# Attention and two expert layers on one core: prologue and first sixteen steps written in another order

## The chip, the cores and the metric

The kernel runs on one core of a Trainium2 chip. The metric is the device time of that core in microseconds (us). Five engines have queues of their own: PE (matrix products), DVE (vector), ACT (activations), POOL, and SP, which here only issues DMAs.

## The reference

Attention over chunks of 32 queries feeds a gated layer and then a layer of eight experts. What the change touches is the attention and the first gated layer:

```python
scores = scale * np.matmul(q_c, k_full.transpose(0, 1, 3, 2))
scores = scores - np.max(scores, axis=-1, keepdims=True)
a = np.exp(scores)
a = a / (np.sum(a, axis=-1, keepdims=True) + 1e-09)
out[:, :, c_start:c_end] = np.matmul(a, v_full)
...
h = x @ w_in
relu6 = np.clip(h + 3.0, 0.0, 6.0)
g = h * relu6 / 6.0
return (g @ w_out).astype(np.float32)
...
for e in range(E):
    h = np.maximum(x @ w1[e], 0.0)
    ye = h @ w2[e]
    out += P[:, e:e + 1] * ye
```

Sizes: 4 batches, 8 heads, 768 positions, 64 per head; 3072 tokens of 512, a hidden layer of 2048 for the first gated layer, and eight experts with 1024 each.

## The kernel before

Attention is cut into 32 **units** u of 96 queries with all eight heads. A unit passes through: a_load and v_load (DMA), a_scores (PE, eight products into two PSUM tiles `sc` of four heads), a_max (DVE, the negated maximum `nm`), a_exp (ACT, eight exponentials, which also give the sums `sm`), a_norm (DVE, `sm`, `rc`, and a multiplication of all of `e`), a_transpose (PE into two PSUM tiles `pt`, ACT copies them to `et`), a_values (PE into `av`) and a_split (ACT `xh`, DVE `xl`: a high and a low part, since every large product is made in three passes). Four units are a block of 384 tokens.

The weights of the first layer arrive as raw 8-byte words and are converted on the core: single_act makes `rest` and `pw` on ACT, single makes `sa` or `sb` with four DVE instructions, single_hi makes the high part `wah`/`wbh` on ACT, and single_lo the low part `wal`/`wbl` on DVE. convert_act(n) holds the ACT half, convert(n) the DVE half (single_lo of what ACT has finished, then single of the next).

The gated layer runs in **steps** i. A step has first(i) (twelve products into `ph`, then `t` on ACT and again on DVE), first_parts(i) (`hh` on ACT, `hl` on DVE) and second(i - 2) (twelve products into four accumulators `pa`). The first 16 steps take two blocks with half the weights, then the same with the other half. Steps 0 to 3 carry a whole unit each; after that a unit is spread over three steps: **turn** marks the step with the transposes, **due** the next one with values, split, scores and maximum.

Everything stands under a manual schedule: each engine executes its instructions in the order in which the code is written. PSUM tiles `pt`, `av` and `sc` of the steps share two banks in turn (`ps_s`), so the second half of a unit's scores needs the bank that its predecessor's `av` held. After the attention, blocks are read back from DRAM by x_load and split by x_split, for the second pass over the layer (`pe` = 1), whose first step begins right after the last step of the first pass.

The prologue of before is:

```python
        for j in range(UPB + 2):
            a_scores(j, True)
            a_load(j + 2)
            if j >= 1:
                a_norm(j - 1)
            if j >= 2:
                a_split(j - 2)
            if j >= 1:
                convert_act(1)
            a_max(j)
            if 1 <= j <= UPB:
                a_transpose(j - 1)
                a_values(j - 1)
                v_load(j + 1)
            a_exp(j)
            convert(1)
```

Of the kernel before, what the change touches and what calls it, by code (L numbers as in the profile page):

```python
# [8 lines left out]
F32 = mybir.dt.float32  # L9
F32R = mybir.dt.float32r  # L10
U32 = mybir.dt.uint32
AF = mybir.ActivationFunctionType
# [5 lines left out]
NH = 8  # L18
# [20 lines left out]
def attn_moe_moe(ctx: ExitStack, tc: tile.TileContext, qk, vw, wi, wo, wa, wb, wg, out):  # L39
# [61 lines left out]
    def raw_load(n):  # L101
        pe, f, t = wide[n]
        raws[n] = at_p.tile([128, 2 * DM], U32, tag="raw", name="raw", bufs=RAW)
        nc.sync.dma_start(out=raws[n], in_=(wi if t == "a" else wo)[pe, f].bitcast(U32))
# [51 lines left out]
    def convert(n):  # L156

        for m in range(going[2], going[1]):
            single_lo(m)
        going[2] = going[1]  # L160
        for m in range(going[0], min(going[0] + n, len(wide))):
            single(m)
            if m + RAW < len(wide):
                raw_load(m + RAW)
            going[0] = m + 1

    def convert_act(n):

        for m in range(going[0], min(going[0] + n, len(wide))):
            single_act(m)  # L170
        for m in range(going[1], going[0]):
            single_hi(m)
        going[1] = going[0]
# [26 lines left out]
    def a_load(u):  # L200
        t = at_p.tile([D + 3, NH, UQ + UK], F32, tag="qk", name="qk", bufs=2)
        nc.sync.dma_start(out=t[:D], in_=qk[u, :D])
        nc.sync.dma_start(out=t[D:], in_=qk[u, D:])
        qk_t[u] = t

    def v_load(u):
        t = at_p.tile([UK, NH * D], F32, tag="vw", name="vw", bufs=2)
        nc.sync.dma_start(out=t, in_=vw[u])
        v_t[u] = t

    def a_scores(u, early=False):

        t = qk_t.pop(u)
        ps, tag = (ps_a, "a") if early else (ps_s, "s")
        sc_t[u] = sc = [ps.tile([UQ, 4, UK], F32, tag=tag, name="sc") for _ in range(2)]
        for h in range(NH):
            nc.tensor.matmul(sc[h // 4][:, h % 4, :], t[:, h, :UQ], t[:, h, UQ:], start=True, stop=True)

    def a_max(u):
        mx = sm_p.tile([UQ, NH], F32, tag="mx", name="mx")  # L220
        for j in range(2):
            nc.vector.tensor_reduce(out=mx[:, 4 * j:4 * j + 4], in_=sc_t[u][j], axis=AX.X, op=ALU.max)
        nm = sm_p.tile([UQ, NH], F32, tag="nm", name="nm")
        nc.vector.tensor_scalar_mul(nm, mx, -SCALE)
        e_t[u] = nm

    def a_exp(u):
        nm, sc = e_t[u], sc_t.pop(u)
        ef = at_p.tile([UQ, NH, UK], F32, tag="e", name="e", bufs=2)
        sm = sm_p.tile([UQ, NH], F32, tag="sm", name="sm")  # L230
        for h in range(NH):
            nc.scalar.activation(
                out=ef[:, h], in_=sc[h // 4][:, h % 4], func=AF.Exp, scale=SCALE, bias=nm[:, h:h + 1],
                accum_out=sm[:, h:h + 1])
        e_t[u] = ef, sm

# [27 lines left out]
    def a_split(u):  # L264
        ps = av_t.pop(u)
        b, i = divmod(u, UPB)
        if i == 0:
            xs[0, b] = x_tiles()
        s = slice(UQ * i, UQ * i + UQ)
        hi, lo = (t[:, :, s] for t in xs[0, b])  # L270
        split(hi, lo, ps)
        xf = at_p.tile([128, KT, UQ], F32, tag="xf", name="xf", bufs=3)
        nc.gpsimd.tensor_tensor(out=xf, in0=hi.bitcast(F32), in1=lo.bitcast(F32), op=ALU.add)
        spills.append((xd[b][:, i], xf))
# [3 lines left out]
    def spill():  # L278
        while spills:
            nc.sync.dma_start(out=spills[0][0], in_=spills.pop(0)[1])  # L280
# [442 lines left out]
    with tc.manual_schedule():  # L723
        at_ctx = pool("at", 2, side="right")
        at_p = at_ctx.__enter__()
        a_load(0)
        v_load(0)
        v_load(1)
        raw_load(0)
        a_load(1)  # L730
        for n in range(1, RAW):
            raw_load(n)
        make_identity(nc, ident)
        nc.gpsimd.memset(ones, 1.0)
# [2 lines left out]


        convert_act(1)
        for j in range(UPB + 2):  # L740
            a_scores(j, True)
            a_load(j + 2)
            if j >= 1:
                a_norm(j - 1)
            if j >= 2:
                a_split(j - 2)
            if j >= 1:
                convert_act(1)
            a_max(j)
            if 1 <= j <= UPB:  # L750
                a_transpose(j - 1)
                a_values(j - 1)
                v_load(j + 1)
            a_exp(j)
            convert(1)

        def rate(i):

            pe, b, f = steps[i]
            return 0 if pe or b == NB1 - 1 else int(i != 4 and i < 11) if i < 2 * NF else f % 2  # L760

        build = None
        jobs, begun = factory(), [0, 0, 0]
        xb_ctx = ctx.enter_context(ExitStack())
        for i, (pe, b, f) in enumerate(steps):


            if i < 4:
                u, turn, due = i + UPB, True, True
            elif i < 2 * NF:  # L770
                u, turn, due = (i - 4) // 3 + 2 * UPB, (i - 4) % 3 == 0, (i - 4) % 3 == 1
            else:
                u, turn, due = (i - 2 * NF) // 2 + 3 * UPB, i % 2 == 0, i % 2 == 1
            turn, due = (pe == 0 and w for w in (turn, due))
            if (pe, b, f) == (0, NB1 - 1, 0):
                at_ctx.__exit__(None, None, None)
                xo_p = ctx.enter_context(pool("xo", 1, side="right"))
            if (pe, b, f) == (1, 1, 0):
                three.close()
                xb_p = xb_ctx.enter_context(pool("xb", 1, side="right"))  # L780
            if (pe, b, f) == (1, NB1 - 1, 0):
                assert build is None and begun[2] == len(jobs)
                xb_ctx.close()
                two.close()
                w1s_p, w1r_p, w2s_p = (
                    ctx.enter_context(pool(n, 1, side="right")) for n in ("w1s", "w1r", "w2s"))
                w1_load(0)
                w2_load(0)
            if (pe, b) == (1, NB1 - 1):
                for do, j in {2: ((w1_hi, 0),), 3: ((w1_lo, 0), (w1_load, 1)), 6: ((w1_hi, 1),),  # L790
                              7: ((w1_lo, 1), (w1_load, 2))}.get(f, ()):
                    do(j)

            for stage_, late in ((2, 4.2), (0, 0), (1, 2)):
                while begun[stage_] < len(jobs) and FIRST_JOB + PERIOD * begun[stage_] + late <= i:
                    jobs[begun[stage_]][stage_]()
                    begun[stage_] += 1
            if pe == 0 and b == NB1 - 1:
                w_load(f)
                if f == 3:  # L800
                    x_load(0)
            if pe == 1 and f == 2:
                x2_load(b)
                if b + 1 < NB1:
                    x_load(b + 1)
            spill()
            first(i)
            if pe or due:
                first_parts(i)
            if turn and due:  # L810
                if i >= LAG:
                    second(i - LAG)
                stage(a_transpose, u)
            if due:
                stage(a_values, u)
                stage(a_split, u)
                convert_act(rate(i))
                stage(v_load, u + 2)
            if i >= LAG and not (turn and due):
                second(i - LAG)  # L820
            if due:
                stage(a_scores, u + 2)
                stage(a_max, u + 2)
                stage(a_exp, u + 2)
                stage(a_load, u + 4)
                stage(a_norm, u + 1)
            if pe == 0 and not due:
                if turn:
                    stage(a_transpose, u)
                first_parts(i)  # L830
                convert_act(rate(i))
            if pe == 0:
                convert(rate(i))
            if later and f in (3, 5, 7):
                gate(*later.pop(0))
            if pe == 0 and b == NB1 - 1 and f >= LAG:
                w_split(f - LAG)
            elif pe == 1 and b == 0 and f < LAG:
                w_split(NF - LAG + f)

            n = b + 1 if pe else 0
            if f >= 4 and n < NB1 and (pe or b == NB1 - 1):
                x_split(n, f - 4)
            if (pe, b, f) == (1, 4, 0):
                build = x_ops(0, xb_p, "xb")
            if build:
                build = build if next(build, 0) is None else None
# [159 lines left out]
```

## Time and profile before

| what | us |
|---|---|
| median of 3 runs | 2633.09 (2632.29 to 2634.93) |
| span of the profiled execution | 2632.3 |
| first product of step 0, step 1, step 4, step 17 (from the span's start) | 42.4, 54.4, 87.2, 167.5 |
| PE busy over the span | 2565.9 |

The span runs from the first instruction to the last. The fastest run took 2632.29 us, so the profiled execution's own time is taken as its span, with nothing worth counting around it. Idle time matters where PE is idle, since PE is busy for 97% of the span; idle time of the others matters only where PE waits for it.

### The profile page before, as it was taken

What the parts mean: (1) busy time and instruction counts of PE and PEld (TensorE: products, weight loads), DVE (VectorE), ACT (ScalarE), POOL (GpSimd) and SP (SyncE); (2) the same over time, 40 slices, a digit from 0 to 9 for tenths busy, and PEclk for the clock granted to TensorE, in tenths of its full rate; (3) what the DMA queues carried; (4) which work ended last, traced back from release to release, by engine and by line L of the source; (5) the groups of instructions that cost most, each with busy time, mean ns of one, the idle gap of its engine ahead of it and who ended that gap; (6) DMA issues with size and microseconds to landing.
All of it is one profiled execution on the core that took longest, in us unless ns stands there. A gap on an engine that the chain in (4) does not pass through costs nothing.

```text
span 2632.3 us, 34096 instructions
## 1 busy us (share of the span) xinstructions
PE 2565.9 (97%) x12725; PEld 2217.9 (84%) x12725; DVE 2140.0 (81%) x2283; ACT 1385.9 (53%) x2323; POOL 1086.1 (41%) x692
## 2 busy tenths in 40 slices
PE   8999999999999999999989999999989999999997
PEld 7899999999977888888868888888868888888886
DVE  6768766556478999998987999998887888898887
ACT  6656654122245555555556555555555655555553
POOL 1034455443005645444433545453433344444442
PEclk9899999999999999999999999999999999999999
DMA  7468868675222443433333334333243333232322
GB/s 201 124 211 266 284 214 278 221 244 192 87 94 92 136 130 112 129 105 107 123 122 119 127 122 136 122 117 106 97 150 110 114 112 98 91 112 98 112 82 75
DMA packets 159702, 366.89 MB, mean 139 GB/s; under 512 B 14352, under 2 KB 75984, under 8 KB 159536
## 3 DMA queue, kind: packets, MB, share of 16 engines
q1 hardware_dynamic: 159536, 364.72, 43.1%
q8 instruction: 100, 1.64, 0.3%
q14 instruction: 66, 0.54, 0.1%
HBM read 297.45 MB, written 67.21 MB: 139 GB/s over the span
## 4 chain that ended last, share of the span: by engine, by line
PE 88%; DVE 6%; DMA 2%; ACT 2%; issue 1%; POOL 1%; SPq 0%; ACTq 0%; DVEq 0%
PE ga L193 6%; PE ga L192 6%; PE ga L194 6%; PE oa L193 6%; PE oa L194 6%; PE oa L192 6%; PE pa L192 3%; PE ph L192 3%; PE oc L193 3%; PE oc L194 3%; PE oc L192 3%; PE ph L193 3%; PE ph L194 3%; PE gc L193 3%; PE gc L192 3%; PE gc L194 3%
## 5 line engine op out<-in xcount | busy, mean ns | idle before, releaser
L637 POOL TENSOR_TENSOR g<-g,pb 128x512 f32<-128x512 f32 x368 | 768.6, 2106 | 1117.4 <-ACT g L630 971.3
L665 ACT ACTIVATE oh<-g 128x1024 fp32r<-128x1024 f32 x336 | 355.3, 1058 | 530.0 <-PE oa L194 178.5
L670 DVE TENSOR_TENSOR ol<-g,oh 128x1024 fp32r<-128x1024 f32 x336 | 493.8, 1481 | 71.4 <-ACT oh L665 71.2
L658 DVE TENSOR_TENSOR g<-g 128x1024 f32<-128x1024 f32 x188 | 323.2, 1752 | 17.9 <-POOL g L637 17.9
L192 PE MATMUL ga<-xo,w1h 128*128 128x512 f32 x768 | 302.3, 394 | 10.3 <-DVE g L624 5.4
L193 PE MATMUL ga<-xo,w1h 128*128 128x512 f32 x768 | 301.0, 392 | 7.2 <-DVE xo L181 7.2
L193 PE MATMUL oa<-ol,w2h 128*128 128x512 f32 x768 | 300.6, 391 | 4.8 <-DVE ol L670 4.8
L192 PE MATMUL oa<-oh,w2h 128*128 128x512 f32 x768 | 300.2, 391 | 0.6 <-ACT oh L665 0.6
L194 PE MATMUL ga<-xo,w1l 128*128 128x512 f32 x768 | 300.1, 391 | 0.0
L194 PE MATMUL oa<-oh,w2l 128*128 128x512 f32 x768 | 300.0, 391 | 0.0
L592 DVE TENSOR_TENSOR w2l<-w2s,w2h 128x1024 fp32r<-128x1024 f32 x168 | 264.6, 1575 | 27.9 <-ACT w2h L586 26.7
L586 ACT ACTIVATE w2h<-w2s 128x1024 fp32r<-128x1024 f32 x168 | 177.6, 1057 | 141.8 <-DMA w2s<-in_wb_dram 76.3
L568 DVE TENSOR_TENSOR w1l<-w1s,w1h 128x1792 fp32r<-128x1792 f32 x96 | 219.0, 2281 | 0.3
L630 ACT ACTIVATE g<-g 128x512 f32<-128x512 f32 x288 | 175.7, 621 | 74.2 <-DVE g L624 73.8
L455 POOL TENSOR_TENSOR fs<-fr 128x256 f32<-128x256 f32 x128 | 110.7, 865 | 212.8 <-DMA ws<-fs 210.0
L306 ACT ACTIVATE t<-ph,half 128x384 f32<-128x384 f32 x128 | 74.5, 582 | 235.2 <-PE ph L194 231.5
L307 DVE SCALAR_TENSOR_TENSOR t<-t,ph 128x384 f32<-128x384 f32 x128 | 70.6, 552 | 139.4 <-ACT t L306 139.3
L192 PE MATMUL ph<-xh,wah 128*128 128x384 f32 x512 | 182.1, 356 | 0.8 <-ACT xh L176 0.8
L192 PEld LDWEIGHTS ga<-xo,w1h 128*128 128x128 f32 x768 | 144.9, 189 | 42.3 <-ACT cp L615 6.2
L193 PE MATMUL ph<-xl,wah 128*128 128x384 f32 x512 | 176.0, 344 | 2.5 <-DVE xl L181 2.4
L193 PEld LDWEIGHTS ga<-xo,w1h 128*128 128x128 f32 x768 | 144.9, 189 | 38.7 <-DVE xo L181 9.5
L193 PEld LDWEIGHTS oa<-ol,w2h 128*128 128x128 f32 x768 | 144.8, 189 | 36.9 <-DVE ol L670 6.8
(140 smaller groups left out, 5904.0 us busy)
## 6 DMA issues: line engine op xcount, KB each, us to landing
w1s<-ws SPq DMA_DIRECT2D x96, 512.0 KB, 4.2
w2s<-ws SPq DMA_DIRECT2D x96, 512.0 KB, 3.9
w1s<-in_wa_dram SPq DMA_DIRECT2D x96, 384.0 KB, 3.1
w2s<-in_wb_dram SPq DMA_DIRECT2D x144, 256.0 KB, 3.3
ws<-fs SPq DMA_DIRECT2D x64, 512.0 KB, 5.8
fr<-in_wa_dram SPq DMA_DIRECT2D x32, 512.0 KB, 5.5
fr<-in_wb_dram SPq DMA_DIRECT2D x32, 512.0 KB, 4.8
qk<-in_qk_dram SPq DMA_DIRECT2D x32, 448.0 KB, 7.9
```

Source lines behind the costliest of these rows:

```text
L192: nc.tensor.matmul(ps, wh, xh, start=start, stop=False, skip_group_check=more)
L193: nc.tensor.matmul(ps, wh, xl, start=False, stop=False, skip_group_check=more)
L194: nc.tensor.matmul(ps, wl, xh, start=False, stop=stop, skip_group_check=more)
L455: nc.gpsimd.tensor_tensor(out=s[o], in0=a, in1=b, op=f)
L568: nc.vector.tensor_tensor(out=lo, in0=w1s.pop(j), in1=w1[j].bitcast(F32), op=ALU.subtract)
L586: nc.scalar.activation(out=hi, in_=w2s[m], func=AF.Copy)
L592: nc.vector.tensor_tensor(out=lo, in0=w2s.pop(m), in1=w2[m].bitcast(F32), op=ALU.subtract)
L630: nc.scalar.activation(out=g, in_=g, func=AF.Relu)
L637: nc.gpsimd.tensor_tensor(out=g, in0=g, in1=p, op=ALU.mult)
L658: eng.tensor_tensor(out=o, in0=gq[n, x, i], in1=gq[n, y, i], op=ALU.subtract)
L665: nc.scalar.activation(out=hi, in_=gq[n, b, i], func=AF.Copy)
L670: nc.vector.tensor_tensor(out=lo, in0=gq[n, b, i], in1=op[m, i].bitcast(F32), op=ALU.subtract)
```

## The change

In the prologue the scores of unit j + 1 are issued before the work on unit j - 1; the maximum of unit j and its exponentials stand ahead of the normalisation of unit j - 1; convert_act now comes behind the exponentials and the transposes, and a_split comes at the end, for unit j - 1 rather than j - 2. The maximum and its scaling are made for each half of the heads apart. Steps 0 to 15 get a function of their own, early. In the last block of the first pass, x_load(0) stands two steps earlier and each x_split one step earlier. The first DMAs have another order.

```diff
     def a_max(u):
-        mx = sm_p.tile([UQ, NH], F32, tag="mx", name="mx")
+        e_t[u] = []
         for j in range(2):
-            nc.vector.tensor_reduce(out=mx[:, 4 * j:4 * j + 4], in_=sc_t[u][j], axis=AX.X, op=ALU.max)
-        nm = sm_p.tile([UQ, NH], F32, tag="nm", name="nm")
-        nc.vector.tensor_scalar_mul(nm, mx, -SCALE)
-        e_t[u] = nm
+            mx = sm_p.tile([UQ, 4], F32, tag="mx", name="mx", bufs=4)
+            nc.vector.tensor_reduce(out=mx, in_=sc_t[u][j], axis=AX.X, op=ALU.max)
+            nm = sm_p.tile([UQ, 4], F32, tag="nm", name="nm", bufs=4)
+            nc.vector.tensor_scalar_mul(nm, mx, -SCALE)
+            e_t[u].append(nm)
...
+        a_scores(0, True)
+        a_load(2)
         for j in range(UPB + 2):
-            a_scores(j, True)
-            a_load(j + 2)
+            a_max(j)
+            a_exp(j)
+            if j < UPB + 1:
+                a_scores(j + 1, True)
+                a_load(j + 3)
             if j >= 1:
                 a_norm(j - 1)
-            if j >= 2:
-                a_split(j - 2)
-            if j >= 1:
-                convert_act(1)
-            a_max(j)
             if 1 <= j <= UPB:
                 a_transpose(j - 1)
                 a_values(j - 1)
                 v_load(j + 1)
-            a_exp(j)
+            if j >= 1:
+                convert_act(1)
             convert(1)
+            if 1 <= j <= UPB:
+                a_split(j - 1)
...
+        def early(i, u, turn, due):
+
+
+            if i < UPB:
+                if i:
+                    a_exp(u + 1)
+                convert(rate(i))
+                first(i)
+                a_transpose(u)
+                a_norm(u + 1)
+                if i >= LAG:
+                    second(i - LAG)
+                a_values(u)
+                a_split(u)
+                first_parts(i)
+                convert_act(rate(i + 1))
+                v_load(u + 2)
+                a_scores(u + 2)
+                a_load(u + 4)
+                a_max(u + 2)
+                return
+            if i == UPB:
+                a_exp(u + 1)
+            if due:
+                a_values(u)
+                a_split(u)
+                v_load(u + 2)
+                a_norm(u + 1)
+            convert(rate(i))
+            first(i)
+            first_parts(i)
+            convert_act(rate(i + 1))
+            second(i - LAG)
+            if due:
+                a_scores(u + 2)
+                a_max(u + 2)
+                a_exp(u + 2)
+                a_load(u + 4)
+            if turn:
+                a_transpose(u)
...
+        convert_act(rate(0))
...
-                if f == 3:
+                if f == 1:
                     x_load(0)
...
             spill()
+            if i < 2 * NF:
+                early(i, u, turn, due)
+                continue
             first(i)
...
-            if f >= 4 and n < NB1 and (pe or b == NB1 - 1):
-                x_split(n, f - 4)
+            r = f - (4 if pe else 3)
+            if 0 <= r < KT and n < NB1 and (pe or b == NB1 - 1):
+                x_split(n, r)
```

The queue of ACT in the prologue, unit j = 2, before: `rest`, `pw` and `wah` are the conversions, `et` the copies of the transposes, `e` the exponentials.

```order
L176 ACTIVATE xh_317<-av_270 128x4x96
L114 ACTIVATE rest_323<-raw_179 128x512
L116 ACTIVATE pw_325<-raw_179 128x512
L139 ACTIVATE wah_327<-sa_293 128x512
L252 ACTIVATE et_334<-pt_335 128x384
L252 ACTIVATE et_334<-pt_341 128x384
L232 ACTIVATE e_358,sm_359<-sc_300,nm_332 96x128 x4
L232 ACTIVATE e_358,sm_359<-sc_301,nm_332 96x128 x4
```

The same queue at the end of unit j = 2 and the beginning of j = 3 in the changed kernel:

```order
L253 ACTIVATE et_360<-pt_367 128x384
L114 ACTIVATE rest_384<-raw_179 128x512
L116 ACTIVATE pw_386<-raw_179 128x512
L139 ACTIVATE wah_388<-sa_312 128x512
L176 ACTIVATE xh_319<-av_373 128x4x96
L233 ACTIVATE e_411,sm_412<-sc_343,nm_405 96x128 x4
L233 ACTIVATE e_411,sm_412<-sc_344,nm_409 96x128 x4
```

The conversions moved from ahead of their unit's exponentials to behind them, with the split's `xh` behind them in turn.

The queue of DVE for j = 2 in the changed kernel: `mx` and `nm` are the maximum, `sm`, `rc` and `e` the normalisation of unit 1, `wal` to `sb` the conversion, `xl` the split of unit 1.

```order
L223 TENSOR_REDUCE mx_325<-sc_263 96x4
L225 TENSOR_SCALAR nm_327<-mx_325 96x4
L223 TENSOR_REDUCE mx_329<-sc_264 96x4
L225 TENSOR_SCALAR nm_331<-mx_329 96x4
L240 TENSOR_SCALAR sm_254<-sm_254 96x8
L242 RECIPROCAL rc_357<-sm_254 96x8
L243 TENSOR_TENSOR e_253<-e_253,rc_357 96x1024
L149 TENSOR_TENSOR wal_390<-sa_312,wah_388 128x512
L125 TENSOR_SCALAR pw_386<-pw_386 128x512
L126 TENSOR_SCALAR sb_392<-pw_386 128x512
L128 SCALAR_TENSOR_TENSOR sb_392<-raw_179,sb_392 128x512
L130 TENSOR_TENSOR sb_392<-sb_392,rest_384 128x512
```

`wal` reads the `wah` that ACT now makes behind the exponentials of j = 2, and the next maximum stands behind the conversion and `xl`; before, the normalisation and `xl` led and the maximum stood directly ahead of the conversion.

The queue of ACT in step 7 (a turn step), before:

```order
L306 ACTIVATE t_1207<-ph_1194,half_95 128x384
L252 ACTIVATE et_1222<-pt_1223 128x384
L252 ACTIVATE et_1222<-pt_1229 128x384
L315 ACTIVATE hh_1235<-t_1207 128x384
L114 ACTIVATE rest_1239<-raw_885 128x512
L116 ACTIVATE pw_1241<-raw_885 128x512
L139 ACTIVATE wah_1243<-sa_1187 128x512
```

And step 7 in the changed kernel:

```order
L307 ACTIVATE t_1255<-ph_1242,half_95 128x384
L316 ACTIVATE hh_1258<-t_1255 128x384
L114 ACTIVATE rest_1262<-raw_928 128x512
L116 ACTIVATE pw_1264<-raw_928 128x512
L139 ACTIVATE wbh_1266<-sb_1235 128x512
L253 ACTIVATE et_1280<-pt_1281 128x384
L253 ACTIVATE et_1280<-pt_1287 128x384
L176 ACTIVATE xh_1088<-av_1293 128x4x96
```

The copies `et` moved from ahead of `hh` and the conversions to behind them. On PE the products first(8) stood between the transposes and the values before; now the values come directly behind the transposes.

## Rows read from the trace of the kernel before

**Rows 1.** The page: span, and the busy time of the engines.

```profile
span 2632.3 us, 34096 instructions
...
PE 2565.9 (97%) x12725; PEld 2217.9 (84%) x12725; DVE 2140.0 (81%) x2283; ACT 1385.9 (53%) x2323; POOL 1086.1 (41%) x692
```

**Rows 2.** Windows: stretch, length, busy PE, PEld, DVE, ACT, POOL, clock, DMA.

```profile
6.00:43.00 37.00, 33.93 (x193) 30.53 (x193) 29.89 (x58) 28.78 (x109) 2.98 (x3) 1.00 0.86 233
...
88.00:168.00 80.00, 74.54 (x482) 72.42 (x481) 52.41 (x98) 46.30 (x146) 13.18 (x16) 0.92 0.49 151
...
430.00:450.00 20.00, 16.75 (x81) 16.18 (x80) 14.50 (x19) 7.82 (x15) 10.72 (x13) 0.83 0.85 298
```

**Rows 3.** Timeline of PE, prologue and steps: start, duration, instruction, idle before.

```profile
32.41 3.73 PE L217 MATMUL sc<-qk 67*96 67x128 f32 x16
36.12 1.51 PE L251 MATMUL pt<-ident,e 96*128 96x96 f32 x8
...
39.05 3.73 PE L217 MATMUL sc<-qk 67*96 67x128 f32 x16
...
43.14 0.69 PE L193 MATMUL ph<-xl,wah 128*128 128x384 f32 x1
...
54.38 0.67 PE L192 MATMUL ph<-xh,wah 128*128 128x384 f32 x1
...
87.16 0.67 PE L192 MATMUL ph<-xh,wah 128*128 128x384 f32 x1
...
167.52 0.42 PE L192 MATMUL ph<-xh,wah 128*128 128x384 f32 x1
```

**Rows 4.** Timeline at the end of the first pass: PE and DVE.

```profile
436.32 0.69 PE L193 MATMUL ph<-xl,wah 128*128 128x384 f32 x1 [2.42 <-DVE xl L181]
...
441.93 0.34 PE L192 MATMUL ph<-xh,wah 128*128 128x384 f32 x1
...
435.20 1.07 DVE L181 TENSOR_TENSOR xl<-xl,xh 128x384 fp32r<-128x384 f32 x1
```

**Rows 5.** Timeline of DVE: a maximum in the prologue, then a whole step.

```profile
10.59 0.17 DVE L224 TENSOR_SCALAR nm<-mx 96x8 f32<-96x8 f32 x1
...
42.54 0.55 DVE L181 TENSOR_TENSOR xl<-av,xh 128x384 fp32r<-128x384 f32 x1
...
54.77 0.69 DVE L222 TENSOR_REDUCE mx<-sc 96x4 f32<-96x512 f32 x1 [1.02 <-PE sc L217]
55.49 0.17 DVE L224 TENSOR_SCALAR nm<-mx 96x8 f32<-96x8 f32 x1
...
57.14 0.68 DVE L149 TENSOR_TENSOR wal<-sa,wah 128x512 fp32r<-128x512 f32 x1
...
60.00 0.55 DVE L307 SCALAR_TENSOR_TENSOR t<-t,ph 128x384 f32<-128x384 f32 x1
61.13 0.56 DVE L318 TENSOR_TENSOR hl<-t,hh 128x384 fp32r<-128x384 f32 x1 [0.59 <-ACT hh L315]
```

**Rows 6.** Timeline of ACT in the prologue: exponentials, conversions, copies of transposes.

```profile
10.86 0.36 ACT L232 ACTIVATE e<-sc,nm 96x128 f32<-96x128 f32 x1 [0.56 <-DVE nm L224]
...
13.62 0.68 ACT L114 ACTIVATE rest<-raw 128x512 uint32<-128x512 uint32 x1
...
34.53 0.69 ACT L114 ACTIVATE rest<-raw 128x512 uint32<-128x512 uint32 x1
...
35.65 0.64 ACT L139 ACTIVATE wah<-sa 128x512 fp32r<-128x512 f32 x1
...
37.03 1.13 ACT L252 ACTIVATE et<-pt 128x384 f32<-128x384 f32 x2 [0.73 <-PE pt L251]
38.06 0.35 ACT L232 ACTIVATE e<-sc,nm 96x128 f32<-96x128 f32 x1
```

**Rows 7.** Timeline of PE in step 6 at full clock: twelve products.

```profile
102.63 0.33 PE L192 MATMUL pa<-hh,wbh 128*128 128x384 f32 x1
...
104.71 0.33 PE L192 MATMUL ph<-xh,wah 128*128 128x384 f32 x1
```

More of the change, by code (lines that the diff above doesn't have):

```diff
@@ L232, in a_exp @@
             nc.scalar.activation(
-                out=ef[:, h], in_=sc[h // 4][:, h % 4], func=AF.Exp, scale=SCALE, bias=nm[:, h:h + 1],
+                out=ef[:, h], in_=sc[h // 4][:, h % 4], func=AF.Exp, scale=SCALE, bias=nm[h // 4][:, h % 4:h % 4 + 1],
                 accum_out=sm[:, h:h + 1])
@@ L726, in attn_moe_moe @@
         a_load(0)
+        a_load(1)
+        raw_load(0)
         v_load(0)
+        raw_load(1)
         v_load(1)
-        raw_load(0)
-        a_load(1)
-        for n in range(1, RAW):
+        for n in range(2, RAW):
             raw_load(n)
```

## Prediction

> **What bounds the kernel now.** The page comes first: PE is busy for 97% of the span [rows 1], so time is won or lost only where PE idles or runs at its lower clock. The windows by stage say where that is: 3.1 us of idle PE in the prologue's 37, 5.5 between 88 and 168, and 3.3 between 430 and 450, where the granted clock is 0.83 [rows 2]; elsewhere PE is full. The timeline of PE gives the pace: in the prologue one unit follows the other by 6.64 us (scores at 32.41 and 39.05), step 0's second product starts at 43.14, step 1 at 54.38, step 4 at 87.16, step 17 at 167.52 [rows 3]. The change acts on nothing behind that but the end of the first pass [rows 4]. So I work out when the changed kernel reaches these marks.
>
> **The prologue.** The rows of order show a loop through two queues that was not there. ACT makes a unit's weight parts (`rest`, `pw`, `wah`) behind its exponentials; DVE's conversion waits for them; the next maximum stands behind the conversion; and the next exponentials wait for that maximum. One turn of the loop, from maximum to maximum:
> half a maximum to `nm` 0.72, `nm` to the first exponential 0.27 [rows 5, 6], eight exponentials 2.76 [rows 6]: 3.75. Meanwhile DVE has done both halves (0.80 each with the small scaling) and the normalisation (1.57, from 55.49 to 57.14 less 0.08 for the scaling [rows 5]), at 3.17; the transposes start some 0.23 later (an estimate: the end of the multiplication and one semaphore), and `et` 0.91 after them (36.12 to 37.03 [rows 3, 6]), at 4.31, so ACT waits 0.56. Then `et` 1.03, `rest` and `pw` 1.12, `wah` 0.65 [rows 6], `wal` and the conversion 2.86 (57.14 to 60.00), `xl` 0.5 [rows 5]. Sum: 10.47 us a unit instead of 6.64. Halving the maximum saves 0.8 of this loop and costs one scaling (0.08 taken; nothing to 0.17, its row's length [rows 5]).
>
> The first maximum of unit 1 comes earlier than now, when DVE has converted the first weight: 10.59 + 0.08 + 2.26 = 12.9 (2.86 less 0.60 for `wal`). The loads are in another order, but the first weight still has about a megabyte of others ahead of it, by the tiles' sizes (two loads of `qk` in place of one and two of `vw`), so I count nothing for that, and 1 us either way for the range. Four turns later, at 12.9 + 41.9 = 54.8, the split of unit 3 is done, and step 0 can start in earnest: 43.14 becomes 54.9, **+11.7**.
>
> **Step 0.** It begins with what the prologue left behind, one after the other: maximum and exponentials of unit 5 (3.75, to 58.6), `rest`, `pw` and a high part (1.77, to 60.3), `wal` and conversion on DVE (2.86, to 63.2), the high part of that (0.65, to 63.8), again 2.86 (to 66.7), `t` 0.55, the normalisation 1.57 and `xl` 0.55 (to 69.4). `xl` frees the bank which the second half of unit 6's scores needs; half of 3.73 [rows 3] later, at 71.2, step 1 starts: 54.38 becomes 71.2, **+16.8** in all.
>
> **Steps 1 to 3.** Here the change helps: the exponentials no longer wait behind this step's scores. Step 1 I take with PE at the lower clock, 1.2 GHz, since it idles before the values of step 0: twelve products at 0.33 (17 from 436.32 to 441.93 [rows 4]) 4.0, transposes 1.5 and scores 3.7 [rows 3], values as the transposes 1.5: 10.7, less a little overlap 10.6. At 2.4 GHz it would be 7.4. Steps 2 and 3 at 2.4 GHz: the exponentials end 3.1 after the scores and free the bank of the second transposes (0.3), second 2.1 (twelve products from 102.63 to 104.71 [rows 7]), values 0.9 (as the transposes of 1.5, at twice the clock), `xh` and `xl` 1.1, half the scores 0.9, semaphores 0.2: 8.6. Sum 27.8 instead of 32.8, **-5.0**; step 4 starts at 99.0.
>
> **Steps 4 to 16.** What stalls now is scores that wait for the bank of `av`, because `xl` stands late on DVE; that goes, with the 5.5 us of idle PE [rows 2]. In its place `et` is late: in a turn step ACT now copies the transposes behind `hh` and the conversions, and PE has nothing between transposes and values. The longest case, from first(5) to first(8): `xh`, `xl` and normalisation 2.7; conversion on DVE 2.3; `t` to `hh` 0.6 (half of the 1.13 from `t` to `hl` [rows 5]); `hh` and the conversions of ACT 2.1; copying four accumulators 1.6 (0.4 each, an estimate by the two copies of `et`); exponentials 2.76; `t` on both engines, to `hh` 1.2; `hh` to the end of the high part 2.2; `wal` and conversion 2.86; `t` to `hh` 0.6; `hh` and conversions 2.1; the first `et` 0.5; values 0.9: 22.4. By the same walk first(4) to first(5) is 7.2, first(8) to first(11) 20.5, where the first product of a new accumulator also waits for the copy, and first(11) to first(17), where no weights are converted, 31.2. Sum 81.3 against 80.4 now [rows 3], **+0.9**. The floor is PE's own work: 13 steps of 24 products at 0.173 are 54.1, and four units' transposes, values and scores at 3.1 are 12.5: 66.6. Work of DVE in the 13 steps is less than that (46), so it sets no bound.
>
> **The end of the first pass.** Now the last `xl` ends at 436.27 and PE has waited for it [rows 4]; 3.25 us of the window are idle [rows 2], and 17 products run at 0.33 instead of 0.173, 2.7 more. With the load two steps and each split one step (over 4 us) earlier, the last `xl` is done near 431, ahead of the eleventh product of that step, which wants it. On SP the load passes two steps' weight loads; its tile is free and its source was written long before, so they are not held up. **-5.9**, at worst 0.
>
> **Sum.** 16.8 - 5.0 + 0.9 - 5.9 = +6.8: 2632.3 + 6.8 = 2639.1 for a profiled execution. The fastest run before equals the span; the median is 0.8 above it, so the median of the changed kernel is forecast at **2639.9**, 0.26% slower.
>
> One rule is weighed here. On ACT a conversion starts at 13.62, right when the eighth exponential is through [rows 6]; I read both queues as strictly in order. The Trainium skill says the same (TensorE: Matmul & The Clock Gate, "Engine queue depths" in Part 1): of the engines only PE reorders, and then only weight loads; ACT and DVE are strict FIFO. Were it otherwise, a conversion could pass the waiting exponentials, the unit would stay at 6.64, and the sum would be 15 us lower, near 2624. The rule speaks against this order of the code.
>
> **The rivals.**
> (a) The values do not wait in steps 4 to 16, because ACT is through with `hh` and conversions when the transposes end. Then PE sets the pace: 66.6 instead of 81.3, and 2639.9 - 14.7 = 2625, faster. The idle DVE in the present steps speaks for it, the chain of waits above against it. It decides the sign where these 13 steps fall below 69; between 69 and 79.9 they leave the whole within 0.2% (5.3 us), which is about what a measurement of this kernel can tell from no change.
> (b) PE stays at 1.2 GHz beyond step 1, or falls back to it after the wait of step 8. A step 2 at that clock is 14.1 instead of 8.6 (4.0 + 1.5 + 4.0 + 1.5 + 3.7, less 0.6 of overlaps): 2645, and up to 2648 with some of step 8. The clock after the wait of only 2.42 us in rows 4 speaks for it. The Trainium skill (same page, "HAM oscillation") has waits that recur and put the array back to the lower clock each time; the trace agrees with 0.33 a product there.
> (c) The earlier split does not help, because DVE is behind in that stretch anyway: 2639.9 + 5.9 = 2646. Its `xl` takes 1.07 there against 0.55 in the prologue [rows 4, 5]; against it, the whole row of splits moves by a step.
>
> **Chances.** The walk as forecast 50% (0.36 slower by over 0.2%, 0.14 within); its 13 steps partly relieved 23% (within); (a) in full 8% (faster); (b) 13% and (c) 6% (slower). Faster 0.08, same 0.37, slower 0.55. The range must reach into the relieved case (3 to 10 us less) and into (b): 2631 to 2648; it leaves out (a) and the far end of (b). The likeliest case alone is 2636 to 2643: step 1 at 2.4 GHz takes 3.2 off, and small errors of the walk are of like size.
>
> **What would show it.** In the profile after: DVE idle by some 3.9 us in each prologue unit before `wal`, with ACT as releaser, and ACT idle as long before the exponentials; units 10.5 apart; step 0's second product near 55, step 1 near 71, step 4 near 99, step 17 near 180; PE waiting 4 to 6 us for `et` before the values of unit 9; no wait for `xl` at the start of the second pass. The prediction is wrong if the prologue's pace stays below 8 (then all falls by 10 or more), or if the 13 steps take 70 or less.

## The result and the profile after

The changed kernel takes **2659.19 us** (median of 4 runs, 2656.40 to 2662.07), the kernel before, on the same chip, 2632.69: the ratio of the runs is **1.0107** (95%: 1.0094 to 1.0120). The forecast was 2639.9 with a range up to 2648: the direction is right, the size is 19 us off. The profiled execution is the longest of the four runs (2662.07).

The page of the changed kernel, span and busy time of the engines; PE is busy 7 us longer than in [rows 1]:

```profile
span 2660.3 us, 34174 instructions
...
PE 2572.8 (97%) x12725; PEld 2215.6 (83%) x12725; DVE 2138.8 (80%) x2315; ACT 1388.6 (52%) x2323; POOL 1083.5 (41%) x692
```

Timeline of PE in the changed kernel: first units, step 0's second product, the first products of steps 1, 2 and 4, the values of unit 9 with two products behind them, and step 17:

```profile
18.73 3.70 PE L217 MATMUL sc<-qk 67*96 67x128 f32 x16 [5.58 <-DMA qk<-in_qk_dram]
22.22 1.49 PE L252 MATMUL pt<-ident,e 96*128 96x96 f32 x8
...
32.91 1.51 PE L252 MATMUL pt<-ident,e 96*128 96x96 f32 x8 [4.05 <-DVE e L243]
...
43.62 1.51 PE L252 MATMUL pt<-ident,e 96*128 96x96 f32 x8 [3.99 <-DVE e L243]
...
54.33 1.51 PE L252 MATMUL pt<-ident,e 96*128 96x96 f32 x8 [3.99 <-DVE e L243]
...
61.50 0.69 PE L193 MATMUL ph<-xl,wah 128*128 128x384 f32 x1 [2.38 <-DVE xl L181]
...
78.34 0.67 PE L192 MATMUL ph<-xh,wah 128*128 128x384 f32 x1
...
85.87 0.42 PE L192 MATMUL ph<-xh,wah 128*128 128x384 f32 x1
...
103.89 0.42 PE L192 MATMUL ph<-xh,wah 128*128 128x384 f32 x1
...
133.26 1.55 PE L261 MATMUL av<-et,vw 128*64 128x96 f32 x16 [5.97 <-ACT et L253]
...
135.22 0.52 PE L193 MATMUL ph<-xl,wah 128*128 128x384 f32 x1
135.54 0.52 PE L194 MATMUL ph<-xh,wal 128*128 128x384 f32 x1
...
186.77 0.42 PE L192 MATMUL ph<-xh,wah 128*128 128x384 f32 x1
```

Read against [rows 3], unit follows unit by 10.71 us in place of 6.64, with PE waiting 4 us for the normalised exponentials each time, and the first unit's transposes (22.22) stand on PE behind scores that waited 5.58 us for a load. The values of unit 9 wait 6 us for `et`.

Timeline of DVE and of ACT in the changed kernel, one wait of each in the prologue: DVE's conversion waits for ACT's `wah`, and ACT's exponentials wait for DVE's `nm`.

```profile
36.62 0.69 DVE L149 TENSOR_TENSOR wal<-sa,wah 128x512 fp32r<-128x512 f32 x1 [3.85 <-ACT wah L139]
...
41.16 0.36 ACT L233 ACTIVATE e<-sc,nm 96x128 f32<-96x128 f32 x1 [4.20 <-DVE nm L225]
```

What PE waited for in the first 700 us of the changed kernel (total, times, longest):

```profile
PE av L261 <- ACT et L253: 14.2, 6, 6.0
PE pt L252 <- DVE e L243: 12.0, 3, 4.1
PE sc L217 <- DMA qk<-in_qk_dram: 11.6, 2, 6.0
PE sc L217 <- DVE xl L181: 3.3, 5, 1.8
```

Windows of the changed kernel, columns as in [rows 2]: the change from the first pass to the second (the product that starts at 436.32 in [rows 4] starts here at 452.14), the way from the second pass to the expert layers, and a stretch of the expert layers.

```profile
450.00:480.00 30.00, 30.00 (x175) 30.00 (x174) 20.53 (x33) 11.19 (x22) 17.68 (x20) 1.00 0.77 267
...
700.00:790.00 90.00, 88.89 (x458) 79.42 (x458) 52.71 (x116) 30.08 (x46) 0.00 (x0) 0.96 0.22 74
...
1000.00:1200.00 200.00, 200.00 (x878) 165.03 (x877) 180.58 (x156) 111.70 (x138) 94.66 (x46) 1.00 0.34 113
```

And the same stretch of the expert layers in the kernel before:

```profile
1000.00:1200.00 200.00, 200.00 (x884) 165.62 (x883) 182.80 (x156) 111.74 (x138) 92.94 (x45) 1.00 0.35 112
```

In both PE is busy all the time at full clock, and yet 878 products are made in place of 884. The groups by line, in that stretch of the changed kernel (busy, mean ns of one); before, each of these means is 389. These are the lengths of the records, which overlap: 200 us for 884 products is one every 226 ns.

```profile
L194 PE MATMUL oa<-oh,w2l 128*128 128x512 f32 x86 | 33.8, 392 | 0.0
L192 PE MATMUL oa<-oh,w2h 128*128 128x512 f32 x86 | 33.6, 391 | 0.0
L193 PE MATMUL oa<-ol,w2h 128*128 128x512 f32 x86 | 33.5, 389 | 0.0
```

The lag of the changed kernel behind the one before is found by pairing equal instructions of both traces, the n-th with the n-th. It is 19.25 us at step 17 (186.77 less 167.52), 13.8 after the end of the first pass, 17.1 where ACT makes the first `w2h` of the expert layers, and 28.6 near the end. Two fifths of the loss (11.5 of 28.0) thus arise where the diff changes no instruction.

### The profile page after: what moved, and what is told of

The parts are those of the page before. It is cut to its first block, busy times and chain, and to the rows that moved or that the text cites. A ratio compares the mean times of both kernels' runs of the same rounds, so it can differ in the third digit from the quotient of the medians.

```text
span 2660.3 us, 34174 instructions
## 1 busy us (share of the span) xinstructions
PE 2572.8 (97%) x12725; PEld 2215.6 (83%) x12725; DVE 2138.8 (80%) x2315; ACT 1388.6 (52%) x2323; POOL 1083.5 (41%) x692
## 4 chain that ended last, share of the span: by engine, by line
PE 88%; DVE 6%; ACT 3%; DMA 2%; issue 1%; POOL 0%; SPq 0%; ACTq 0%; DVEq 0%
PE ga L194 6%; PE ga L192 6%; PE ga L193 6%; PE oa L194 6%; PE oa L193 6%; PE oa L192 6%; PE gc L194 3%; PE gc L192 3%; PE oc L194 3%; PE gc L193 3%; PE oc L192 3%; PE oc L193 3%; PE pa L192 3%; PE ph L192 3%; PE pa L194 3%; PE pa L193 3%
## 5 line engine op out<-in xcount | busy, mean ns | idle before, releaser
L671 DVE TENSOR_TENSOR ol<-g,oh 128x1024 fp32r<-128x1024 f32 x336 | 487.2, 1462 | 76.7 <-ACT oh L666 76.6
```

What stands on the lines that cost most here:

```text
L671: nc.vector.tensor_tensor(out=lo, in0=gq[n, b, i], in1=op[m, i].bitcast(F32), op=ALU.subtract)
```

## The experiments

Theory A said: the halves of `mx` and of `nm`, four buffers of 16 bytes for each that take 32 bytes a buffer, put all tiles behind them at the left end of SBUF 128 bytes further (`w2h` from 3808 to 3936), and that makes products slower. Rivals: the expert layers go slower because they start later, or because of the order of instructions. Theory B: the rest is the prologue's loop and the first unit.

**Addresses alone.** pad_only is the kernel before with the shift and nothing else; after_old_addr is the changed kernel without the shift.

```diff
+    sm_p.tile([UQ, 16], F32, tag="pad", name="pad")      # pad_only
     ident = const.tile([128, 128], F32, name="ident")
```
```diff
-            mx = sm_p.tile([UQ, 4], F32, tag="mx", name="mx", bufs=4)
+            mx = sm_p.tile([UQ, 4], F32, tag="mx", name="mx")      # after_old_addr; nm too
```

> The kernel before, with 128 more bytes per partition reserved in the pool of small tiles, so that the tiles behind it stand where the changed kernel has them; no instruction moves. In the expert layers the changed kernel loses about 11.5 us in 1800 although PE waits no longer there: each third product takes a few ns more. Theory A (the shift of the tiles by 128 bytes does it): about 11 to 12 us slower than before, mean product of the expert layers 391 ns. Theory B (the order or number of PE's instructions does it): no change, 389 ns. Theory C (it is the run or the chip, not the kernel): 389 ns and no change here, and the changed kernel at its old addresses may show either.

> The changed kernel with two buffers in place of four for the halved maximum and its scaling, so that all other tiles stand at the addresses of before. Theory A (addresses): the expert layers run as before (389 ns a product), and the time is some 11 us below the changed kernel's: near 2647. Theory B (instructions): near 2659 and 391 ns. The first 190 us should be those of the changed kernel in either case (step 17 near 187).

pad_only: 2642.62 us, ratio 1.0041 (1.0028 to 1.0054); its lag is -0.2 at the start of the expert layers and grows evenly to 11.7. after_old_addr: 2646.38, ratio 1.0054 (1.0041 to 1.0068), and 884 products in the window again; its lag is 14.3 from the end of the first pass to the start of the expert layers and 13.6 at their end. So the shift costs 11.0 us by pad_only (2642.62 less the 2631.63 of the kernel before, measured beside it) and 12.8 by after_old_addr (2659.19 less 2646.38). The order of the code costs 14.8 (2646.38 less 2631.63) or the 13.7 that are left of 26.5. Theory A holds.

**What about the address.** Three other shifts of the kernel before, by the same line with other sizes; then 32 bytes that move only tiles of the expert layers (all those at the left end, or those behind the second weights); and 32 bytes at the left with 224 at the right.

```diff
-        w2r_p, g_p, op_p, y_p, pb_p, tmp_p, out_p = (
+        w2r_p, pad_p, g_p, op_p, y_p, pb_p, tmp_p, out_p = (      # pad_32_behind
...
+        pad_p.tile([128, 8], F32, tag="pad", name="pad")
```
```diff
+    sm_p.tile([UQ, 8], F32, tag="pad", name="pad", bufs=1)      # pad_both
+    ctx.enter_context(pool("padr", 1, side="right")).tile([128, 56], F32, tag="padr", name="padr")
```

> The kernel before with one unused tile of 32 bytes ahead of all others, so that the tiles behind it stand 32 bytes further (with 128 bytes the span was 10.5 us longer, products 391/389/392 ns instead of 389). Theory of alignment: the pace of products hangs on where a tile begins within some block of bytes; 32 bytes bring the weights from 3808 to 3840, a multiple of 256, so that the pace is another than at 128, as before or faster: 2625 to 2633. Rival, the distance: what counts is that the tiles stand nearer to or further from those at the right end, which don't move; then any shift is slower, 32 bytes by a part of it or by the whole: 2634 to 2643.

> The same with 256 bytes. If the place of a tile within 256 bytes (or a divisor of it above 128) decides: products at 389, the time that of before, 2630 to 2633. If the place within 512 bytes decides, or the distance to the tiles at the right end: products at 391 or another pace, 2638 to 2650.

> The same with 512 bytes. If the place of a tile within 512 bytes or within a divisor of it decides: products at 389, 2630 to 2633. If the distance to the tiles at the right end decides: slower than with 128 bytes or the same, 2640 or more.

> The kernel before with the unused 32 bytes only in the expert layers, ahead of all their tiles at the left end. If the slower products come from tiles of the expert layers: slower by 20 us, 2648 to 2655, as with 32 bytes ahead of everything. If from the small tiles ahead of them (the identity, the half, the routing's rows): 2630 to 2633.

> The same, with the 32 bytes behind the second weights (w2h, w2l), so that these stay at 3808 and g, oh, ol, y and what follows move. If the second weights against the tiles at the right end decide: as before, 2630 to 2633. If the moved operands oh and ol, or what DVE, ACT and POOL write, decide: slower, 2640 to 2655. If only the difference between tiles that are used together counts, oh against w2h now differ as well, and it may be slower than with 32 bytes ahead of all.

> The kernel before with 32 unused bytes at the left end and 224 at the right, so that all tiles of the expert layers stand at a multiple of 256 bytes. If only the difference in place between tiles at the left and at the right counts: products at 389 again, 2629 to 2634. If the place itself counts: slower, as with 32 bytes at the left alone or worse, 2645 to 2670.

The start of each tile is known from the built program; its remainder by 256 stands in the table, with the products in the window from 1000 to 1200:

| run | `w2h` | `oh`, `g` | `xo`, `w1h` | products | ratio (95%) |
|---|---|---|---|---|---|
| before | 224 | 224 | 224 | 884 | 1 |
| pad_only | 96 | 96 | 224 | 878 | 1.0041 (1.0028 to 1.0054) |
| pad_32 | 0 | 0 | 224 | 871 | 1.0081 (1.0063 to 1.0100) |
| pad_256 | 224 | 224 | 224 | 884 | 1.0002 (0.9992 to 1.0011) |
| pad_512 | 224 | 224 | 224 | 884 | 1.0006 (0.9995 to 1.0018) |
| pad_32_expert | 0 | 0 | 224 | 872 | 1.0084 (1.0064 to 1.0104) |
| pad_32_behind | 224 | 0 | 224 | 863 | 1.0150 (1.0134 to 1.0165) |
| pad_both | 0 | 0 | 0 | 884 | 1.0002 (0.9991 to 1.0013) |

The same groups by line as above, first of pad_32_behind, then of pad_both:

```profile
L192 PE MATMUL oa<-oh,w2h 128*128 128x512 f32 x86 | 34.2, 398 | 0.0
L193 PE MATMUL oa<-ol,w2h 128*128 128x512 f32 x86 | 33.8, 393 | 0.0
L194 PE MATMUL oa<-oh,w2l 128*128 128x512 f32 x85 | 33.7, 397 | 0.0
```
```profile
L194 PE MATMUL oa<-oh,w2h 128*128 128x512 f32 x88 | 34.2, 389 | 0.0
L195 PE MATMUL oa<-ol,w2h 128*128 128x512 f32 x88 | 34.2, 389 | 0.0
L196 PE MATMUL oa<-oh,w2l 128*128 128x512 f32 x88 | 34.2, 389 | 0.0
```

pad_32 met neither of its two expectations: it is slower by 22 us, twice as much as pad_only. The place itself does not count: at 0 throughout products take 389 ns as at 224 throughout. What counts in these runs is that the tiles in use together stand at the same place within 256 bytes. In pad_32, where `oh` and `w2h` moved together, their products are slow too (394 ns), so it isn't only a product's own two operands.

The traces hold the start of each product in ns, and these show where the time goes. PE makes products in groups of six, in turn of the experts' first layer (into `ga`, `gb`, `gc`) and of the second (into `oa`, `ob`, `oc`). In the kernel before, between 1000 and 1200 us, each starts 226 or 227 ns after the one before it. In the changed kernel so do those inside a group; but from the first product of a group to the second it is 230 or 231 ns, and from the last to the next group 232 or 233, in all 73 groups of either layer. It is the same, to 0.2 ns in the mean, whether ACT, POOL or a DMA is at work at that moment or not. So PE does not lose this time to another engine or a transfer: it loses it in its own accesses, in the changed kernel where it goes from tiles at 96 to tiles at 224 and back. Which two accesses of PE get in each other's way stays open: in pad_32 some products inside a group of the second layer are slow too, though all its tiles are at 0 (235 or 236 ns from the fourth to the fifth).

**The prologue.** convert_ahead is the changed kernel (with the shift) and ACT's weight parts ahead of the exponentials; values_first has the old addresses, and a unit's scores behind the values of the unit before; repaired is values_first and convert_ahead together.

```diff
             a_max(j)
+            if j >= 1:
+                convert_act(1)      # convert_ahead
             a_exp(j)
-            if j < UPB + 1:
-                a_scores(j + 1, True)
-                a_load(j + 3)
...
                 v_load(j + 1)
+            if j < UPB + 1:
+                a_scores(j + 1, True)      # values_first
+                a_load(j + 3)
-            if j >= 1:
-                convert_act(1)
```

> The changed kernel with the prologue's conversions on ACT put ahead of the unit's exponentials again; all else as changed. Loop theory (conversions behind exponentials close a loop of 10.5 us through ACT and DVE): units 7.5 us apart in place of 10.7, step 0's second product near 50 in place of 61.5, total some 11 us less. Rival (the loads of qk and the raw weights pace the prologue): units stay above 10.

> The changed kernel with tiles at the old addresses (2646.4 us, step 0's second product at 61), and in the prologue a unit's scores put behind the transposes and values of the unit before. Theory: in the first unit the transposes stand on PE behind the scores of unit 2, which wait for their load until 18.4, while the normalised exponentials are ready at 16.4; so transposes near 16.5, next maximum near 23.5 in place of 28.9, units still 10.5 to 10.7 apart, step 0's second product near 56 and the median 5 to 6 us below that kernel's, near 2641. Rival: the prologue starts from the load of unit 2's scores whatever stands behind it; then the second product stays at 61 and the time within 1 us of 2646.

> The changed kernel with its three losses taken out: tiles at the old addresses, scores behind the values of the unit before, and ACT's weight parts ahead of the exponentials in the prologue. Theory: these are the whole loss; then step 0's second product is at 45 or 46 in place of 61.5, the gains of steps 1 to 3 and of the pass's end show, and the median is 2624 to 2629. Rival: another loss stands behind them (steps 4 to 16 take 88 or more, or the second pass is longer); then 2631 or more.

convert_ahead: 2644.09 us, ratio 1.0053 (1.0037 to 1.0068); units 7.79 apart and step 0's second product at 50.27: the loop is the one forecast. values_first: 2639.89, ratio 1.0029 (1.0018 to 1.0041), 6.5 below after_old_addr; step 0's second product is at 56.03 (61.17 there), units are still 10.7 apart. In its timeline of PE the first transposes are no longer behind the scores of unit 2:

```profile
16.76 1.51 PE L252 MATMUL pt<-ident,e 96*128 96x96 f32 x8 [3.78 <-DVE e L243]
...
19.69 3.73 PE L217 MATMUL sc<-qk 67*96 67x128 f32 x16
...
27.47 1.51 PE L252 MATMUL pt<-ident,e 96*128 96x96 f32 x8 [4.04 <-DVE e L243]
```

repaired missed its expectation: 2633.36, ratio 1.0000 (0.9990 to 1.0009), not 2624 to 2629. Its timeline of PE shows why:

```profile
26.00 1.51 PE L252 MATMUL pt<-ident,e 96*128 96x96 f32 x8 [2.63 <-DVE e L243]
...
28.99 3.73 PE L217 MATMUL sc<-qk 67*96 67x128 f32 x16
...
35.35 1.51 PE L252 MATMUL pt<-ident,e 96*128 96x96 f32 x8 [2.63 <-DVE e L243]
```

Units are 9.35 apart, and step 0's second product is at 51.54, not at 45 or 46. The normalisation stands on DVE behind the next unit's maximum, so transposes wait for scores that are now issued behind the transposes and values before them: 1.5, 1.5, 3.7 and 2.6 of waiting make the turn. With the conversions out of the way this loop is the longer one; neither theory had it, and the two remedies do not add. The rival that was named had the time (2631 or more) but not the place.

**Steps 4 to 16 and the rest.** et_ahead (old addresses) puts a unit's transposes right behind the first products of a step; old_prologue_et has, besides, the prologue and loads of before; old_but_four is the kernel before with the new order in steps 0 to 3 and at the end of the first pass alone (these three, too, make the maximum by halves, at the old addresses); pass_end_only is the kernel before with the last of these.

```diff
             first(i)
+            if turn:
+                a_transpose(u)      # et_ahead
             first_parts(i)
...
-            if turn:
-                a_transpose(u)
```
```diff
-            if i < 2 * NF:
+            if i < UPB:      # old_but_four
                 early(i, u, turn, due)
                 continue
+            if i == UPB:
+                a_exp(u + 1)
```
```diff
-                if f == 3:
+                if f == 1:      # pass_end_only; each x_split a step earlier as in the change
                     x_load(0)
```

> The changed kernel with tiles at the old addresses, and in steps 4 to 16 a unit's transposes put right behind the first product, ahead of the copies and conversions that ACT makes for that step. Theory: PE waits there for the copied transposes, because ACT makes them behind its other work of the step (6.0 us before the values of unit 9 in the changed kernel, 82.9 us for the 13 steps); then that wait goes, the 13 steps take 72 to 77, and the median falls to 2636 to 2641. Rival: ACT and DVE are short of time in these steps as a whole; then the wait moves to the products that need the converted weights or to the next exponentials, the 13 steps stay at 80 or more, and the time within 3 us of 2646.

> As the run with the transposes ahead in steps 4 to 16, but with the prologue and the order of loads of the kernel before. Theory: the prologue's loop and the first unit's wait cost 19 to 20 us by step 17, and the new order of steps 1 to 3, that of the pass's end and the transposes ahead bring some 5, 6 and 6: step 0's second product near 43, units 6.6 apart, step 17 near 158 to 162, median 2614 to 2620. Rival: the new order of the steps needs the prologue that goes with it (the exponentials a unit ahead), so that the waits return in steps 0 to 4: step 17 at 168 or later and the median 2625 or more.

> The kernel before with the new order in steps 0 to 3 alone and the earlier splits at the end of the first pass. Theory: steps 1 to 3 gain 5 us beside the old prologue too, and the pass's end 6: step 4 near 82 in place of 87, median 2620 to 2624. Rival: the gain of steps 1 to 3 is given back in the old steps 4 to 16 (their waits for the bank of the values are the same work later): median near 2625, that of the earlier splits alone.

> The kernel before with nothing but the earlier load and splits at the end of the first pass. My term of the prediction: 5.9 us faster (2626.5 to 2627.5), PE without a wait for xl at the start of the second pass. Rival: the waits move to the next place on DVE, and the gain is below 2 us.

et_ahead: 2645.05, ratio 1.0046 (1.0031 to 1.0060), not to be told from after_old_addr. What PE waits for in its 13 steps (79.8 us, from 104.01 to 183.81):

```profile
PE pa L192 <- ACT x L351: 3.5, 2, 3.1
PE pt L252 <- ACT e L233: 2.8, 3, 1.2
PE av L261 <- ACT et L253: 0.8, 1, 0.8
```

The 6 us wait is gone, but PE now stands before ACT's copies of the accumulators and the exponentials: the steps are 3.1 us shorter where 6 to 11 were expected. old_prologue_et: 2621.62, ratio 0.9960 (0.9944 to 0.9976), a little over the 2614 to 2620 expected, and **old_but_four: 2620.61, ratio 0.9954 (0.9940 to 0.9969)**, the lowest median of all, though not to be told from the run just named. Step 4 and step 17 in the timeline of PE of old_but_four; in old_prologue_et they begin at 81.91 and 160.82:

```profile
81.83 0.42 PE L192 MATMUL ph<-xh,wah 128*128 128x384 f32 x1
...
160.82 0.42 PE L192 MATMUL ph<-xh,wah 128*128 128x384 f32 x1
```

So the new order of steps 0 to 3 gains 5.3 us without its prologue (81.83 against 87.16), and steps 4 to 16 take 79 in the old order and in the new one with the transposes ahead. pass_end_only: 2625.30, ratio 0.9975 (0.9966 to 0.9984): at the end of the first pass its lag falls from -2.3 to -8.4.

## Why the prediction was wrong

| stage | forecast | measured, profiled execution |
|---|---|---|
| to step 0's second product | +11.7 | +18.4 (43.14 to 61.50) |
| to step 1, sum | +16.8 | +24.0 (54.38 to 78.34) |
| steps 1 to 3 | -5.0 | -7.2 (25.55 in place of 32.78) |
| steps 4 to 16 | +0.9 | +2.5 (82.88 in place of 80.36) |
| end of the first pass | -5.9 | -5.5 |
| from there to the expert layers | 0 | +3.3 |
| expert layers | 0 | +11.5 |

The measured column takes one execution of each kernel. In steps 4 to 16, which pad_only and pass_end_only leave as they were, the old order took 80.4, 78.7 and 77.3 us; the changed order took 82.9 to 83.2 in five runs (the changed kernel, after_old_addr, convert_ahead, values_first, repaired). So it costs 2.5 to 5.9 there, not 2.5 for certain.

**The largest miss: "Halving the maximum saves 0.8 of this loop and costs one scaling (0.08 taken...)".** The instructions were costed, their tiles weren't, and so "The change acts on nothing behind that but the end of the first pass" failed: it put the expert layers at 0. The shift by 128 bytes is worth +11.5 in the profile and +11.0 to +12.8 between medians.

**The second: "so I count nothing for that, and 1 us either way".** I asked when the first weight arrives, not when the load for the scores of unit 2 does, behind which the first unit's transposes now stand on PE. So the first turn, from `nm` to `nm` on DVE (13.93 to 29.94), takes 16.0 us in place of 10.47, 5.5 more. values_first takes 5.1 of this back (from 61.17 in after_old_addr to 56.03); what then remains over the 54.9 forecast is 1.1, and four turns at 10.71 in place of 10.47 are 1.0 of it.

**The loop of the prologue** was right in mechanism and size, and convert_ahead confirms it: without conversions behind the exponentials a turn falls to 7.79. The Trainium skill (TensorE: Matmul & The Clock Gate, "Engine queue depths" in Part 1) has ACT and DVE strictly in order; the trace agrees: at 10.71 us a unit no conversion passed an exponential.

**Step 0** was forecast at 16.3 from its second product to step 1 and took 16.8. **Steps 1 to 3:** step 1 was taken wholly at 1.2 GHz, 10.6, and took 7.5: its products are 0.32 apart only until 80.4 and 0.17 after. Steps 2 and 3 took 9.0 each, forecast 8.6.

**Steps 4 to 16:** the wait of the values of unit 9 came as forecast, 5.97 us where 4 to 6 stood. Rival (a), no such wait, fell. Its floor of 66.6 was too low as well: PE is busy for 72.0 of the 82.9 us, in part because some of them run at the lower clock (mean 0.96), and with the wait removed, in et_ahead, the steps still take 79.8. Rival (b) fell in its first half: 9.0 for step 2 is no step at 1.2 GHz (14.1). Its second half came true: behind the wait of unit 9's values products are 0.32 us apart (135.22 and 135.54 in the timeline above) until 138.4 and 0.17 after, with a granted clock of 0.50, the lower of its two levels (1.2 GHz), from 133 to 136.

**The end of the first pass:** the window from 450 to 480 is full at clock 1.00, where before 16.75 of 20 us were busy, at 0.83 [rows 2]; rival (c) fell. The wait for `xl` of [rows 4] is gone.

**The 3.3 us from the second pass to the expert layers** come with a fall of the clock. The window from 700 to 790 has a granted clock of 0.96 there and 1.00 in after_old_addr, whose lag stays at 14.3. Neither the shift nor the new order is needed for it: pad_256, which has the instructions and the pace of the kernel before, falls back by 3.1 us in the same place (lag -1.9 to 1.2, granted clock 0.66 from 725 to 735), and pad_only by half of that (-1.8 to -0.2, 0.83). So it most likely belongs to the execution and not to the change; what sets it off is open.

With the two missed terms (5.1 to 5.5 and 11.0 to 12.8) the forecast of 2639.9 would have been 2656 to 2658. What is left is smaller and has both signs (step 1 took 3.1 us less than forecast, the way to the expert layers 3.3 more), so that the sum then comes so near 2659 is in part luck.

## What to carry to other kernels

Here a change that resized small tiles moved every large tile behind them: compare the start addresses of large operands within 256 bytes before and after, however small the tile is; here 16-byte tiles cost nearly as much as the whole reordering. When work is issued earlier on an in-order engine, ask of each item passed what it now waits for, loads included, from the first turn on. And a wait that has been seen is not worth its length: in steps 4 to 16 the waits for `et` fell from 9.2 us in all to 0.8 and 3.1 were gained, since what stood behind them was nearly as late.

## What the runs showed of the hardware

PE's pace in these runs depends on where its tiles stand relative to each other in SBUF. With all large tiles of the expert layers at the same place within 256 bytes a product of 128x512 takes 389 ns; with the left ones 128 bytes off 389 to 393, 32 bytes off 388 to 395, and with `w2h` and `oh` 32 bytes apart as well up to 398, all with PE never idle and at full clock. The two passes ahead of the expert layers, whose products read tiles at the left alone, which move together, kept their pace: 1200 products between 500 and 700 us in pad_only, 1201 before.

The Trainium skill (SBUF — State Buffer, "SBUF: two separate sides") says that PE, ACT and DVE's own ports never wait on anyone. As far as the other engines and the transfers go, the traces agree: the slow products take the same time beside a busy ACT, POOL or DMA as beside an idle one (to 0.2 ns). But PE is not free of where its own tiles stand: placement alone changed the number of products in 200 us by up to 2.4% (884 to 863), and the ratio of the whole kernel by 1.5%. That the tiles PE reads decide fits pad_32_expert and pad_32_behind: between them only the second weights `w2h` and `w2l` move, and the kernel is 15.6 us slower (2655.69 to 2671.27).
